# Float32 bits of the float64 weights built in a contiguous tile, mask constants loaded first, and 96-row value loads, in an attention-plus-two-mixtures kernel

## The chip, the cores and the metric

One NeuronCore of a Trainium2 chip runs the whole kernel as one launch. The metric is device time in microseconds (us): the time of one execution, as the median of three runs. The engines are TensorE (PE, matrix products), VectorE (DVE), ScalarE (ACT), GpSimd (POOL) and SyncE (SP, which here only issues DMAs).

## The reference

Three stages follow one another. First sparse attention over 4 batches, 8 heads, 576 positions and head width 64; heads 0 to 3 see a band of 32 positions (local), heads 4 to 7 see every 32nd position (strided). Then a gated two-layer product with float64 weights, and then a mixture of eight experts of which each token uses two. Cut to what matters:

```python
mask_local = (rel >= 0) & (rel < stride)
mask_strided = (rel >= 0) & (pos[None, :] % stride == pos[:, None] % stride)
attn = softmax(np.where(mask, scale * q @ k.T, -1e9))     # per head
x = (attn @ v).transpose(0, 2, 1, 3).reshape(2304, 512)
h = x @ w_in                                   # 512 x 2048, float64
x = (h * (1.0 / (1.0 + np.exp(-1.702 * h)))) @ w_out      # 2048 x 512, float64
# second mixture: 8 experts of 512 x 1024 and 1024 x 512, top 2 of noisy logits per token
out[mask] += top2_w[mask, k, None] * (np.maximum(x[mask] @ w1[e], 0.0) @ w2[e])
```

## The kernel before

The 2304 tokens run in six chunks of 384 (`c`). A prologue loop (lines 698 to 712) computes most of the first batch's attention; then the loop over `(c, fc)` (lines 747 to 797) runs the first mixture with 16 slices of 128 hidden units (`fc`) for each chunk, and works on attention groups of later chunks and on other tasks in between. From line 801 on, the second mixture runs per expert. In the first part the order on PE, ACT, DVE and POOL is the order in which the program writes the instructions (`manual_schedule`, lines 118 and 682); only the order of SP's DMA issues is left to the scheduler.

**The float64 weights.** Each piece of 128x512 float64 weights is loaded as pairs of 32-bit words into `raw` (`w_raw`, called `area` or `raw` in the trace; four such buffers). `w_bits` makes float32 bits of it with three DVE instructions: line 387 shifts and masks the high words into a tile `cv`; line 390 shifts the low words and joins them with `cv`, written back over the low words, that is into every second word of `raw`; line 393 adds sign and exponent bits, again into every second word. Then `w_split` makes two float32r parts: ACT copies the result (line 362, the high part), POOL subtracts (line 363, the low part). The `cv` tile has one buffer and is free after line 390. `raw` is free after line 363. Wide pieces have 512 columns (28 of them); the last two `fc` have eight pieces of 256 columns.

**How the pieces pass.** `w_step` is a generator: each `next(conv)` lets out the next of the three DVE instructions. One `fc` iteration of chunk 0 holds two such steps, the first half (lines 758 to 769) and the second half (lines 770 to 795). Each half ends with `w_split`, which issues the ACT copy and the POOL subtraction of the step before the one just finished (`SPLIT` holds two lists). So the POOL subtraction of step k stands at the end of step k+1, and line 387 of step k+2 is the next DVE instruction of a step after it. In the prologue only every second pass holds a step (`CONVAT`), while every pass calls `w_split`.

**Order on the engines in one iteration of chunk 0.** DVE: line 387 (first half), line 418 (gate product, from PSUM), line 193 (low part of attention values), line 390, line 169 (masked scores, two), line 393; line 387 (second half), line 178, line 390, line 180 (normalisation), line 393. POOL: line 425 (low part of the gate), line 363 of the last second-half step, line 182 (normalised probabilities), line 363 of this iteration's first-half step. ACT: line 416 (tanh), line 190, line 423 (high part of the gate), line 174 (exponents), line 362, line 240 (copy of the transposed probabilities), line 362.

**Loads and constants.** `chained` (line 138) gives DMAs to SP one behind another. The constants `cs` (128x738 float32: identity, local masks, strided mask and others) are one DMA, second in the queue, between the first group's `qk` and its `v`. A local group's `v` is a 128x384 load of which the product reads 96 rows (line 252). A tile `zero` of 128x512, filled by POOL at line 720 ahead of chunk 0, is the source with which `clear` writes zeros to DRAM during chunks 3 and 4.

Of the kernel before, what the change touches and what calls it, by code (L numbers as in the profile page):

```python
# [9 lines left out]
F32 = mybir.dt.float32  # L10
F32R = mybir.dt.float32r
BF16 = mybir.dt.bfloat16
I32 = mybir.dt.int32
# [9 lines left out]
DM = H * D  # L23
# [32 lines left out]
WAIT1 = 15  # L56
R_PP = R_LG + 16 * TPC

C_ID = 0
C_ML = C_ID + 128  # L60
C_MS = C_ML + 2 * KW
C_TRI = C_MS + 128
C_TOK = C_TRI + 128
C_EB = C_TOK + NT
# [33 lines left out]
def tile_kernel(ctx, tc, qkL, qkS, vL, vS, wm1, wm2, wgn, noise, cst, lst0, out):  # L98
# [19 lines left out]
    with ExitStack() as main, tc.manual_schedule(engines={mybir.EngineType.PE}):  # L118
# [13 lines left out]
        def xtile(c):  # L132
            X[c] = xtp.tile([128, 2, 4, CH], F32R, tag="xt", name=f"xt{c}")

        # ---------------- attention
        LASTLD = {}

        def chained(dst, src, late=False):
            prev = LASTLD.get(late) or LASTLD.get(False)
            if prev is None:  # L140
                ins = nc.sync.dma_start(dst, src).ins
            else:
                with tc.issue_after(prev):
                    ins = nc.sync.dma_start(dst, src).ins
            LASTLD[late] = ins

        def attn_load(gr, early):
            b, pr, g = gr
            if early:
                area = wp.tile([128, 2048], F32, tag="w", name="att")  # L150
                qk, v = area[:, :QKL], area[:, QKL:QKL + 384].rearrange("p (t d) -> p t d", d=128)
                p, pt = area[:, 1024:1408], area[:, 1408:1792]
            else:
                qk = ldp.tile([128, QKL], F32, tag="qk", name="qk", bufs=2)
                v = ldp.tile([128, 3, 128], F32, tag="v", name="v", bufs=3)
                p = pt = None
            if pr < 2:
                chained(qk, qkL[b, pr, g], not early)
                if (b, pr, g) == (0, 0, 0):
                    chained(cs, cst)  # L160
                chained(v, vL[b, pr, g].rearrange("p (t d) -> p t d", d=128), not early)
            else:
                chained(qk[:, :QKS], qkS[b, pr - 2, g], not early)
                chained(v[:, 0, :], vS[b, pr - 2, g], not early)
            return qk, v, p, pt
# [108 lines left out]
            put_x(parts, conv)  # L274

        class Attention:
            """Groups in order, each in four stages; a group starts once it lies below `limit`."""

            def __init__(self, gs, early, pooled):
                self.gs, self.early, self.pooled = gs, early, pooled  # L280
# [36 lines left out]
                    g_av(self.gs[i], self.ld[i], self.pt.pop(i), banks[i % len(banks)], conv)  # L317
                    self.done += 1

        # ---------------- float64 weights: bits -> float32 -> two float32r parts  # L320
        W1 = {}

        PIECES, SMALL, held, born, done, slot = [], [], [], [], [], {}
        SPLIT = [[], []]

        def w_raw(fc, s):
            """Load a part of the weights of fc and, with the first, make room for the result."""
            if fc >= NFC:
                return
            wide = fc < NFC - 2  # L330
            if wide:
                if not s:
                    slot[fc] = wslot(f"w1_{fc}")
                w = slot[fc][:, :, 512 * s:512 * s + 512]
            else:
                w = rap.tile([128, 2, 512], F32R, tag="ra", name=f"w1_{fc}_{s}")
            W1[fc, s] = w[:, 0, :], w[:, 1, :]
            if wide:
                raw = rap.tile([128, 512, 2], I32, tag="ra", name="area")
                chained(raw.rearrange("p n t -> p (n t)"), wm1[fc, :, 512 * s:512 * s + 512].bitcast(I32))  # L340
                PIECES.append((fc, s, raw, 0, 512))
            else:
                SMALL.extend((fc, s, o, 256) for o in (0, 256))
# [12 lines left out]
                born.append(len(done))  # L356

        def w_split():
            """float32r parts of what the step before converted"""
            for fc, s, w32, o, n in SPLIT.pop(0):  # L360
                hi, lo = W1[fc, s]
                nc.scalar.copy(hi[:, o:o + n], w32)
                nc.gpsimd.tensor_sub(lo[:, o:o + n], w32, hi[:, o:o + n].bitcast(F32))
                if n < 512:
                    held.pop()
                else:
                    w_raw(fc + 2, s)
            w_small()
            SPLIT.append([])
            done.append(0)  # L370

        def w_step():
            left = 512
            while PIECES and left:
                fc, s, raw, o, n = PIECES[0]
                if n < 512:
                    if len(done) < born[0] + LATE:
                        return
                    born.pop(0)
                PIECES.pop(0)  # L380
                left -= n
                yield from w_bits(fc, s, raw, o, n)

        def w_bits(fc, s, raw, o, n):
            t = tmp.tile([128, n], I32, tag="cv", name="cv", bufs=1)
            low, high = raw[:, :, 0], raw[:, :, 1]
            nc.vector.tensor_scalar(t, high, 3, 0x3FFFFFFF,
                                    op0=OP.logical_shift_left, op1=OP.bitwise_and)
            yield
            nc.vector.scalar_tensor_tensor(low, low, 29, t,  # L390
                                           op0=OP.logical_shift_right, op1=OP.bitwise_or)
            yield
            nc.vector.scalar_tensor_tensor(low, high, -0x40000000, low,
                                           op0=OP.bitwise_and, op1=OP.bitwise_or)
            SPLIT[-1].append((fc, s, low.bitcast(F32), o, n))
            yield

        # ---------------- first mixture: two products with a gated activation
        GT = {}
        LASTMM = [None]  # L400

# [35 lines left out]
                m = nc.tensor.matmul(o, g[:, 1, a], w[0], start=False, stop=(fc == NFC - 1))  # L437
            LASTMM[0] = m.ins

        # ---------------- routing  # L440
        scat = []

        def routing(c, tb, lb, wait=3):
# [72 lines left out]
            nc.tensor.matmul(ps, ones, mc, start=True, stop=False)  # L516
            nc.tensor.matmul(ps[:, :TPC], tri, mb[:, :TPC], start=False, stop=True)
            nc.scalar.copy(pp, ps)
            # weights of the two experts
            pay = one.tile([128, TPC, 2, 2], F32, tag="pay", name="pay", bufs=2)  # L520
            sc = one.tile([128, 8, TPC], F32, tag="sc", name="sc")
            for k in range(2):
# [6 lines left out]
            nc.vector.tensor_scalar(sc[:, 3], sc[:, 2], 1.0, 1e-9, op0=OP.add, op1=OP.add)  # L529
            nc.vector.reciprocal(pay[:, :, 0, 1], sc[:, 3])  # L530
            nc.vector.tensor_mul(pay[:, :, 1, 1], sc[:, 2], pay[:, :, 0, 1])
            # places in the experts' lists
            pos, t1 = sm[:, 10], sm[:, 11]
            nc.vector.tensor_add(pos, pp[:, :TPC], base[:, None, :].to_broadcast([128, TPC, E]))
            nc.vector.tensor_add(base, base, pp[:, TPC])
# [15 lines left out]
                    scat.append(s)  # L551
            yield

        # ---------------- second mixture: per expert
        W2 = {}

        def w2_load(h):
# [112 lines left out]
                    tc.declare_no_dep(s.ins, o.ins, reason="an expert's tokens are distinct")  # L670
                adds[e].append(s)

        # ================= program
        def groups(b, loc):
            return [(b, pr, g) for pr in (0, 1, 2, 3) for g in (loc if pr < 2 else range(NG))]

# [39 lines left out]
        nc.vector.memset(ones, 1.0)  # L716
        nc.vector.tensor_copy(base, cs[:, C_EB:C_EB + E])

        z = one.tile([128, DM], F32, tag="zero", name="zero")
        nc.gpsimd.memset(z, 0.0)  # L720

        def clear(t, r0, n):
            src = bass.AP(tensor=z.tensor, offset=z.offset, ap=[list(z.ap[0]), [0, n], [1, DM]])
            chained(t[r0:r0 + 128 * n, :].rearrange("(b p) d -> p b d", p=128), src, True)

        fill = []

        def step(n=1):
            for _ in range(n):
# [18 lines left out]
        for i, (c, fc) in enumerate(seq):  # L748
            if fc == 0:
                if c:  # L750
                    drain()
                for k in {2: (3, 4), 3: (5,)}.get(c, ()):
                    xtile(k)
                if 0 < c < len(parts):
                    finish(c)
                if c + 1 < len(parts):
                    att.limit = upto[c + 1]
            conv = w_step()
            t, g = m1_l1(c, fc, step, conv)
            att.values([7])  # L760
            att.transposes([6])
            next(conv, None)
            att.scores([5])
            next(conv, None)
            m1_split(c, t, g)
            att.exps()
            for _ in conv:
                pass
            w_split()
            conv = w_step()  # L770
            att.norms(conv)
            if c == 3 and fc in (4, 6, 8, 10, 12):
                clear(x2d, 64 * fc - 256, 1)
            if c == 0 and fc == 12:
                chained(lst.rearrange("(p n) t -> p (n t)", p=128),
                        lst0.rearrange("(p n) t -> p (n t)", p=128), True)
            if c == 4 and fc % 2:
                clear(out, CH * (fc // 2), min(TPC, NT + NBLK - TPC * (fc // 2)))
            if c == NCHUNK - 1 and fc == 6:
                drain()  # L780
                e_list(0, 0, NA // 128)
                fill.append(e_part(0, 0, N + DUMP - CH, wait=WAIT0))
            if c == NCHUNK - 1 and fc >= 8:
                w2_load(fc - 8)
            if i:
                m1_l2(*seq[i - 1], step)
                if fc == 0:
                    fill.insert(0, routing(c - 1, [6], 7))
            att.values([7], conv)
            next(conv, None)  # L790
            att.transposes([6])
            att.load()
            for _ in conv:
                pass
            w_split()
            if (c, fc) == (NCHUNK - 2, NFC - 1):
                fine.close()
# [49 lines left out]
                m2_l2(h, (t,))  # L847
            e_out(E - 1, (t,))

        # ---------------- blocks beyond the fixed capacity  # L850
        ov = one.tile([1, 6, E], F32, tag="ov", name="ov")
        oi = one.tile([1, E], I32, tag="oi", name="oi")
        nc.vector.tensor_sub(ov[:, 0], base[0:1], cs[0:1, C_EB:C_EB + E])
# [119 lines left out]
```

## Time and profile before

| | us |
|---|---|
| median of three runs | 1048.15 |
| lowest and highest of three | 1048.09, 1048.95 |
| span of the profiled execution | 1046.7 |
| PE busy | 999.4 (95%) |
| DVE busy | 498.7 (48%) |
| ACT busy | 394.7 (38%) |
| POOL busy | 233.0 (22%) |

The profile is of one execution; its span, from the first to the last instruction, lies 1.45 us under the median. Busy times are totals over stages with different limits, so they are read stage by stage: by windows of time, by the order of instructions in one loop iteration, and by what each engine waited for. A busy instruction on DVE or POOL can be one that has started and stands still; its duration against the shortest of its kind shows that.

### The profile page before, as it was taken

To read this page: it belongs to the slowest core of one execution; us is meant where nothing else is said; L and a number is where in the kernel's file an instruction comes from. 1 tells how busy PE (TensorE), PEld (TensorE's weight loads), DVE (VectorE), ACT (ScalarE), POOL (GpSimd) and SP (SyncE) were. 2 spreads that over 40 slices of the span, in tenths; PEclk is the share of its full clock that TensorE was granted. 3 is DMA by queue.
4 is the path that set the end of the run, shared out by engine and by line. 5 is a ranking of instruction groups with operands and counts; after the bars stand their busy time and mean duration, and the time that the engine had idled before them with its cause. 6 is when DMAs were issued, how large, how long until landed. Compare 5 with 4: busy or idle time off the path is not lost. (4 is left out here: it accounts for less than half of the span.)

```text
span 1046.7 us, 16112 instructions
## 1 busy us (share of the span) xinstructions
PE 999.4 (95%) x5804; PEld 884.2 (84%) x5804; DVE 498.7 (48%) x1509; ACT 394.7 (38%) x1075; POOL 233.0 (22%) x210
## 2 busy tenths in 40 slices
PE   6898799999999999999989999999999999999996
PEld 5776688998888888889978779998999998999995
DVE  5999955236544744522553454343434334343311
ACT  5754444234435444322343153242423323233311
POOL 2577630200200200110210333032220405031302
PEclk9699999999999999999989999999999999999998
DMA  8656521011212223400050065253452726253403
GB/s 278 217 179 191 188 73 48 1 62 46 51 53 87 78 88 129 180 1 31 31 188 34 19 183 153 81 118 124 88 155 81 164 78 145 97 132 111 93 9 51
DMA packets 64352, 107.69 MB, mean 103 GB/s; under 512 B 13056, under 2 KB 26496, under 8 KB 64256
## 3 DMA queue, kind: packets, MB, share of 16 engines
q1 hardware_dynamic: 54160, 85.64, 25.4%
q0 software_dynamic: 10112, 21.02, 10.1%
q8 instruction: 46, 0.75, 0.3%
q14 instruction: 34, 0.28, 0.1%
HBM read 84.04 MB, written 22.73 MB: 102 GB/s over the span
## 5 line engine op out<-in xcount | busy, mean ns | idle before, releaser
L638 DVE SCALAR_TENSOR_TENSOR ht<-pb,ht 128x384 fp32r<-128x384 f32 (+1 forms) x128 | 62.5, 488 | 254.9 <-ACT ht L637 254.9
L637 ACT ACTIVATE ht<-pb 128x384 fp32r<-128x384 f32 (+1 forms) x128 | 56.0, 438 | 264.7 <-PE pb L636 264.6
L411 PE MATMUL pb<-xt,w 128*128 128x384 f32 x384 | 135.8, 354 | 0.0
L666 POOL DMA_INDIRECT out<-y,ix x40 | 65.3, 1633 | 290.4 <-ACT y L665 260.9
L412 PE MATMUL pb<-xt,w 128*128 128x384 f32 x384 | 129.5, 337 | 0.1
L413 PE MATMUL pb<-xt,w 128*128 128x384 f32 x384 | 129.6, 337 | 0.0
L435 PE MATMUL pb<-w,g 128*128 128x512 f32 x288 | 121.1, 420 | 7.5 <-ACT g L423 7.5
L650 PE MATMUL pb<-w,ht 128*128 128x512 f32 x320 | 127.8, 399 | 0.0
L651 PE MATMUL pb<-w,ht 128*128 128x512 f32 x320 | 125.3, 392 | 0.0
L652 PE MATMUL pb<-w,ht 128*128 128x512 f32 x320 | 125.1, 391 | 0.0
L546 POOL DMA_INDIRECT lst<-pay,si x36 | 36.2, 1004 | 399.1 <-DVE si L543 338.6
L418 DVE SCALAR_TENSOR_TENSOR th<-th,pb 128x384 f32<-128x384 f32 x96 | 52.9, 551 | 148.9 <-ACT th L416 148.8
L437 PE MATMUL pb<-w,g 128*128 128x512 f32 x288 | 115.8, 402 | 0.6 <-POOL g L425 0.6
L436 PE MATMUL pb<-w,g 128*128 128x512 f32 x288 | 114.8, 399 | 0.0
L416 ACT ACTIVATE th<-pb 128x384 f32<-128x384 f32 x96 | 47.0, 490 | 140.7 <-PE pb L413 138.6
L564 DVE TENSOR_TENSOR w<-raw,w 128x512 fp32r<-128x512 f32 x128 | 83.9, 688 | 15.7 <-ACT w L563 15.3
L634 PE MATMUL pb<-xa,w 128*128 128x384 f32 x256 | 87.2, 340 | 0.0
L636 PE MATMUL pb<-xa,w 128*128 128x384 f32 x256 | 86.3, 337 | 0.0
L635 PE MATMUL pb<-xa,w 128*128 128x384 f32 x256 | 86.0, 336 | 0.0
L423 ACT CAST g<-th 128x384 fp32r<-128x384 f32 x96 | 49.3, 513 | 87.7 <-DVE th L418 87.5
L563 ACT CAST w<-raw 128x512 fp32r<-128x512 f32 x128 | 73.9, 617 | 16.3 <-DMA raw<-wm 16.2
L412 PEld LDWEIGHTS pb<-xt,w 128*128 128x128 f32 x384 | 72.9, 190 | 2.5 <-DVE st L178 0.4
(167 smaller groups left out, 1999.0 us busy)
## 6 DMA issues: line engine op xcount, KB each, us to landing
raw<-wm SPq DMA_DIRECT2D x136, 256.0 KB, 3.0
area<-wm SPq DMA_DIRECT2D x28, 512.0 KB, 4.0
out<-zero SPq DMA_DIRECT2D x7, 768.0 KB, 6.9
qk<-qkS SPq DMA_DIRECT2D x28, 189.0 KB, 2.8
qk<-qkL SPq DMA_DIRECT2D x16, 304.0 KB, 2.9
x2d<-row SPq DMA_DIRECT2D x15, 256.0 KB, 2.2
v<-vL SPq DMA_DIRECT2D x16, 192.0 KB, 2.4
att<-qkL SPq DMA_DIRECT2D x8, 304.0 KB, 6.2
```

The costliest lines, as they stand in the source:

```text
L411: nc.tensor.matmul(ps, w[0][:, a], X[c][:, 0, kc, :], start=(kc == 0), stop=False)
L412: nc.tensor.matmul(ps, w[0][:, a], X[c][:, 1, kc, :], start=False, stop=False)
L413: nc.tensor.matmul(ps, w[1][:, a], X[c][:, 0, kc, :], start=False, stop=(kc == 3))
L435: nc.tensor.matmul(o, g[:, 0, a], w[0], start=(fc == 0), stop=False)
L436: nc.tensor.matmul(o, g[:, 0, a], w[1], start=False, stop=False)
L437: m = nc.tensor.matmul(o, g[:, 1, a], w[0], start=False, stop=(fc == NFC - 1))
L634: nc.tensor.matmul(ps, w[:, 0, a], x[:, 0, kc, :], start=(kc == 0), stop=False)
L635: nc.tensor.matmul(ps, w[:, 0, a], x[:, 1, kc, :], start=False, stop=False)
L636: nc.tensor.matmul(ps, w[:, 1, a], x[:, 0, kc, :], start=False, stop=(kc == 3))
L650: nc.tensor.matmul(o, g[:, 0, a], w[:, 0, 512:], start=(fc == 0), stop=False)
L651: nc.tensor.matmul(o, g[:, 0, a], w[:, 1, 512:], start=False, stop=False)
L652: m = nc.tensor.matmul(o, g[:, 1, a], w[:, 0, 512:], start=False, stop=(fc == NF2 - 1))
```

## The change

- `w_step` takes one `cv` tile of 128x512 for a step, from two buffers that take turns (the pool's default) where there was one. `w_bits` writes all three results into a contiguous slice of that tile. `raw` is only read, by DVE. The ACT copy and the POOL subtraction read the `cv` tile, so it is in use until line 363's subtraction is done, and `raw` until the third DVE instruction.
- The local masks stand first in `cs`; their columns load ahead of the first `v`, the other columns behind it, in a DMA of their own.
- A local group's `v` loads 96 rows.
- The `zero` tile becomes a `cv` tile, filled at the start of chunk 3.
- Comments and blank lines go.

```diff
-C_ID = 0
-C_ML = C_ID + 128
-C_MS = C_ML + 2 * KW
+C_ML = 0
+C_ID = C_ML + 2 * KW
+C_MS = C_ID + 128
...
                 if (b, pr, g) == (0, 0, 0):
-                    chained(cs, cst)
-                chained(v, vL[b, pr, g].rearrange("p (t d) -> p t d", d=128), not early)
+                    chained(cs[:, :C_ID], cst[:, :C_ID])
+                chained(v[:KW], vL[b, pr, g, :KW].rearrange("p (t d) -> p t d", d=128), not early)
+                if (b, pr, g) == (0, 0, 0):
+                    chained(cs[:, C_ID:], cst[:, C_ID:])
...
             for fc, s, w32, o, n in SPLIT.pop(0):
-                hi, lo = W1[fc, s]
-                nc.scalar.copy(hi[:, o:o + n], w32)
-                nc.gpsimd.tensor_sub(lo[:, o:o + n], w32, hi[:, o:o + n].bitcast(F32))
+                hi, lo = (w[:, o:o + n] for w in W1[fc, s])
+                nc.scalar.copy(hi, w32)
+                nc.gpsimd.tensor_sub(lo, w32, hi.bitcast(F32))
...
-            left = 512
+            left, t = 512, None
...
+                if t is None:
+                    t = tmp.tile([128, 512], I32, tag="cv", name="cv")
+                yield from w_bits(fc, s, raw, o, n, t[:, 512 - left:512 - left + n])
                 left -= n
-                yield from w_bits(fc, s, raw, o, n)
-
-        def w_bits(fc, s, raw, o, n):
-            t = tmp.tile([128, n], I32, tag="cv", name="cv", bufs=1)
+
+        def w_bits(fc, s, raw, o, n, w32):
             low, high = raw[:, :, 0], raw[:, :, 1]
-            nc.vector.tensor_scalar(t, high, 3, 0x3FFFFFFF,
+            nc.vector.tensor_scalar(w32, high, 3, 0x3FFFFFFF,
                                     op0=OP.logical_shift_left, op1=OP.bitwise_and)
             yield
-            nc.vector.scalar_tensor_tensor(low, low, 29, t,
+            nc.vector.scalar_tensor_tensor(w32, low, 29, w32,
                                            op0=OP.logical_shift_right, op1=OP.bitwise_or)
             yield
-            nc.vector.scalar_tensor_tensor(low, high, -0x40000000, low,
+            nc.vector.scalar_tensor_tensor(w32, high, -0x40000000, w32,
                                            op0=OP.bitwise_and, op1=OP.bitwise_or)
-            SPLIT[-1].append((fc, s, low.bitcast(F32), o, n))
+            SPLIT[-1].append((fc, s, w32.bitcast(F32), o, n))
...
-        z = one.tile([128, DM], F32, tag="zero", name="zero")
-        nc.gpsimd.memset(z, 0.0)
...
+                if c == 3:
+                    ZERO.append(tmp.tile([128, DM], F32, tag="cv", name="zero"))
+                    nc.gpsimd.memset(ZERO[0], 0.0)
```

## Rows read from the trace of the kernel before

**Rows 1.** The page: the span, and DVE's busy tenths in 40 slices of the span (26 us each).

```profile
span 1046.7 us, 16112 instructions
...
DVE  5999955236544744522553454343434334343311
```

**Rows 2.** Busy time of each engine in two stretches: most of chunk 0, and from the end of chunk 0 to the end of the span. Columns: stretch, its length, busy us (instructions) of PE, PE's weight loads, DVE, ACT, POOL, granted clock, DMA share, GB/s.

```profile
46.00:126.00 80.00, 68.41 (x417) 56.60 (x416) 79.03 (x173) 40.92 (x128) 57.79 (x47) 0.98 0.56 182
...
142.00:1046.00 904.00, 883.66 (x5118) 789.15 (x5116) 372.66 (x1151) 318.40 (x804) 148.04 (x126) 0.99 0.32 88
```

**Rows 3.** The timeline of DVE and POOL in one iteration of chunk 0. Columns: start us, duration us, engine, line, operation, tiles, shapes, count, and in brackets the idle time before it with what ended it.

```profile
69.04 0.42 DVE L387 TENSOR_SCALAR cv<-area 128x512 int32<-128x512 int32 x1
...
69.38 0.15 DVE L178 TENSOR_SCALAR st<-st 126x2 f32<-126x2 f32 x1
69.45 1.30 POOL L363 TENSOR_TENSOR w<-area,w 128x512 fp32r<-128x512 f32 x1 [0.88 <-ACT w L362]
...
69.56 1.73 DVE L390 SCALAR_TENSOR_TENSOR area<-area,cv 128x512 int32<-128x512 int32 x1
...
71.22 0.15 DVE L180 RECIPROCAL st<-st 126x2 f32<-126x2 f32 x1
...
71.33 0.69 DVE L393 SCALAR_TENSOR_TENSOR area<-area 128x512 int32<-128x512 int32 x1
71.45 1.04 POOL L182 TENSOR_TENSOR psd<-psd,st 126x252 f32<-126x252 f32 x1 [0.70 <-DVE st L180]
...
71.94 0.83 DVE L387 TENSOR_SCALAR cv<-area 128x512 int32<-128x512 int32 x1
...
72.45 1.50 POOL L363 TENSOR_TENSOR w<-area,w 128x512 fp32r<-128x512 f32 x1
...
72.69 0.54 DVE L418 SCALAR_TENSOR_TENSOR th<-th,pb 128x384 f32<-128x384 f32 x1
...
73.16 0.45 DVE L193 TENSOR_TENSOR xt<-pb,xt 128x42 fp32r<-128x42 f32 x2
...
73.50 0.99 DVE L390 SCALAR_TENSOR_TENSOR area<-area,cv 128x512 int32<-128x512 int32 x1
...
73.90 1.47 POOL L425 TENSOR_TENSOR g<-th,g 128x384 fp32r<-128x384 f32 x1
...
74.42 0.28 DVE L169 CUSTOM_DVE_ANT_0 psd<-pb,cs 126x126 f32<-126x126 f32 x1
```

**Rows 4.** The same iteration's end: DVE's timeline, and the POOL subtraction that closes it.

```profile
74.84 1.08 DVE L393 SCALAR_TENSOR_TENSOR area<-area 128x512 int32<-128x512 int32 x1
75.84 0.41 DVE L387 TENSOR_SCALAR cv<-area 128x512 int32<-128x512 int32 x1
...
76.25 1.30 POOL L363 TENSOR_TENSOR w<-area,w 128x512 fp32r<-128x512 f32 x1 [0.88 <-ACT w L362]
```

**Rows 5.** Timelines of DVE and POOL: the first and the last line 387 of chunk 0's steps whose counterpart two steps back is still running on POOL, and that counterpart, line 363.

```profile
51.73 0.62 DVE L387 TENSOR_SCALAR cv<-area 128x512 int32<-128x512 int32 x1
...
120.20 1.78 DVE L387 TENSOR_SCALAR cv<-raw 128x256 int32<-128x256 int32 x1
...
52.03 1.48 POOL L363 TENSOR_TENSOR w<-area,w 128x512 fp32r<-128x512 f32 x1
...
120.53 1.30 POOL L363 TENSOR_TENSOR w<-area,w 128x512 fp32r<-128x512 f32 x1
```

**Rows 6.** All instructions of one line over the whole span. Columns: engine, operation, tiles, count, shortest, median and longest ns, first and last start, shapes. Lines 390, 393 and 363 work on every second word of `raw`; lines 425 and 564 on contiguous tiles.

```profile
L390 DVE SCALAR_TENSOR_TENSOR area<-area,cv x28: 675/1082/1831, 14.5 to 118.9; 128x512 int32<-128x512 int32 x28
...
L393 DVE SCALAR_TENSOR_TENSOR area<-area x28: 692/694/1194, 15.2 to 119.6; 128x512 int32<-128x512 int32 x28
...
L564 DVE TENSOR_TENSOR w<-raw,w x128: 679/691/694, 518.9 to 989.1; 128x512 fp32r<-128x512 f32 x128
...
L363 POOL TENSOR_TENSOR w<-area,w x28: 1291/1306/1504, 18.2 to 124.0; 128x512 fp32r<-128x512 f32 x28
...
L363 POOL TENSOR_TENSOR w<-raw,w x8: 742/773/919, 125.5 to 141.0; 128x256 fp32r<-128x256 f32 x8
...
L425 POOL TENSOR_TENSOR g<-th,g x16: 998/1458/1472, 48.2 to 143.8; 128x384 fp32r<-128x384 f32 x16
```

**Rows 7.** Who waited for whom, 0 to 160 us, on SP (us in total, times, longest); and the timeline row of the first conversion, with the one wait of line 387 for its data.

```profile
SPq L144 <- POOL w L363: 70.2, 23, 7.7
...
13.70 0.43 DVE L387 TENSOR_SCALAR cv<-area 128x512 int32<-128x512 int32 x1 [0.81 <-DMA area<-wm]
```

**Rows 8.** The start: PE's wait for the second group's `qk` in the timeline, the size of a local group's `v` load in the list of DMA issues (KB each, median us from issue to landing), and the DMA rate between 6 and 8 us (columns as in rows 2).

```profile
7.59 4.35 PE L206 MATMUL pb<-att 128*128 128x96 f32 x18 [2.49 <-DMA att<-qkL]
...
att<-vL SPq DMA_DIRECT2D x8, 192.0 KB, 6.1
...
6.00:8.00 2.00, 0.41 (x2) 0.41 (x3) 0.00 (x0) 0.77 (x5) 0.00 (x0) 1.00 1.03 371
```

**Rows 9.** The end of chunk 0's conversions: a line 387 on DVE, and on POOL the three merged subtractions of which the second is its counterpart two steps back.

```profile
131.34 1.10 DVE L387 TENSOR_SCALAR cv<-raw 128x256 int32<-128x256 int32 x1
...
132.25 2.37 POOL L363 TENSOR_TENSOR w<-raw,w 128x256 fp32r<-128x256 f32 x3
```

**Rows 10.** PE's longest idle time inside chunk 0's strided groups, and the granted clock just after it (columns as in rows 2).

```profile
90.71 0.35 PE L262 MATMUL pb<-pt,v 72*64 72x72 f32 x4 [2.14 <-ACT pt L240]
...
92.00:94.00 2.00, 2.00 (x6) 1.56 (x6) 2.00 (x5) 0.00 (x0) 1.35 (x2) 0.50 0.49 152
```

More of the change, by code (lines that the diff above doesn't have):

```diff
@@ L717, in tile_kernel @@
         nc.vector.tensor_copy(base, cs[:, C_EB:C_EB + E])
-        z = one.tile([128, DM], F32, tag="zero", name="zero")
-        nc.gpsimd.memset(z, 0.0)
         def clear(t, r0, n):
+            z = ZERO[0]
             src = bass.AP(tensor=z.tensor, offset=z.offset, ap=[list(z.ap[0]), [0, n], [1, DM]])
             chained(t[r0:r0 + 128 * n, :].rearrange("(b p) d -> p b d", p=128), src, True)
-        fill = []
+        fill, ZERO = [], []
         def step(n=1):
```

## The prediction

> **What bounds the kernel now.** I read the share of busy time by stretches first, then the order of instructions in one loop iteration, then the shortest and median durations of single lines, and last the waits. The share alone says "PE, 95%"; the slices say more: DVE is at nine tenths or above from slice 2 to slice 5, roughly 26 to 130 us, and at half after that [rows 1]. In 46 to 126 us DVE is busy 79.03 of 80 us, while PE, whose busy time includes overlapping matmuls, has 68.41; from 142 us on PE is busy 884 of 904 us [rows 2]. So the kernel has a first part whose pace DVE sets and a second whose pace PE sets. A delay in the first part starts the second later, and nothing there can take it back.
>
> What the reader is to see in one iteration of the first part [rows 3, 4]: its period is 76.25 - 69.45 = 6.80 us, and DVE has no gap, but several of its instructions stand still. Line 390 takes 1.73 us at 69.56 though its shortest run is 0.68 [rows 6]: POOL's line 363 runs to 70.75, and line 390 ends 0.54 later. Line 387 at 71.94 ends 0.28 after POOL's line 182; the next line 390 (0.99) ends 0.54 after POOL's line 363. The other way round, line 182 at 71.45 ends 0.47 after DVE's line 393. Such DVE and POOL instructions take turns. While POOL subtracts, DVE goes on only with what needs no turn: lines 418 and 193 run through POOL's 72.45 to 73.95.
>
> **Part 1, the contiguous tile: what it removes.** Strided operands seem to cost DVE nothing: line 393 on every second word has a median of 694 ns, line 564 on contiguous tiles 691, both 128x512 [rows 6]. On POOL the line through 742 ns (256 columns) and 1291 (512) gives 1017 at 384; the contiguous line 425 has 998 at its shortest [rows 6]. The gain is 0.02 us a subtraction, and I put it at nothing. `raw` comes free after DVE's third instruction instead of POOL's subtraction, so SP issues weight loads earlier; SP waited 70.2 us on line 363 for that, but the converting line 387 waited for data just once, 0.81 us at 13.70, before any buffer is used again [rows 7]. Nothing.
>
> **What it adds.** The result stays in the `cv` tile until POOL has subtracted, and there are two such tiles. So line 387 of step k+2 must wait for line 363 of step k. In program order that subtraction is issued only at the end of step k+1, and line 387 of step k+2 is DVE's next conversion. In the rows, line 387 at 69.04 starts 1.71 us before its counterpart ends (69.45 + 1.30), the one at 71.94 starts 2.01 before the other ends (72.45 + 1.50) [rows 3]. The first such pair is 51.73 against 52.03 + 1.48, the last 120.20 against 120.53 + 1.30 [rows 5]: two waits an iteration, ten iterations. In the prologue a pass without conversion lies between, in which POOL subtracts, so I count none. Queued behind the waiting line 387 on DVE are the normalisation (lines 178, 180), which POOL's line 182 waits for, and line 418, which ACT's line 423 and then POOL's line 425 wait for.
>
> **The new period, step by step**, from T, the end of the second-half step's counterpart on POOL (70.75 in the rows); hand-over 0.08 (line 180 ends 71.37, line 182 starts 71.45), all from [rows 3, 4] and unblocked lengths from [rows 6]:
> - line 387 at T+0.08; line 390 0.52 after it begins (69.04 to 69.56), 0.69 long, ends T+1.29 (now T+0.54, since line 387 had run under the subtraction);
> - line 393 0.04 later, 0.69 long: T+2.02; line 182, blocked by it, 0.47 more: T+2.49;
> - line 363 of the first half starts 0.04 before that and takes 1.30 with no DVE in its way: T+3.75;
> - only now the next line 387, T+3.83, 0.42 long; line 418 starts 0.08 before it ends: T+4.17; line 390 starts 0.81 after line 418: T+4.98; ends T+5.67 (now T+3.74);
> - from there to the next line 363 as now, 76.25 - 74.49 = 1.76 (masks, exponents, ACT's copy): T+7.43; its 1.30: T+8.73.
>
> 8.73 instead of 6.80 is 1.93 us an iteration: the work that ran under POOL's subtractions, lines 387, 418 and 193, now follows them. Bounds: 1.4, if line 182 gets its turn before line 393 (saves about 0.45) and the hand-over is shorter; 2.4, if line 393 of the first half, which ends about 0.3 ahead of line 363 in this count, slips in front of it. I take 1.93, which follows the program order.
>
> Sum over the stage: the first waiting line 387 ends at 52.03 + 1.30 + 0.08 + 0.42 = 53.83 (now 52.35). Ten periods later it is 141.1; less 0.8, an estimate, for two iterations whose group has 72 rows instead of 126 [rows 10]: 140.3. Now that instruction ends at 120.20 + 1.78 = 121.98 [rows 5]. So +18.3 us. In the tail, line 387 at 131.34 would wait for the second of three subtractions that start at 132.25, till about 133.8 [rows 9]: 0 to 1.4 us; I take 0.3, nearer to nothing, since the last slices' products come later.
>
> **Part 2, masks first.** The first group's masks come earlier, but PE waits for the second group's `qk` until 7.59, which stands behind the same constants [rows 8]. Nothing; bounds 0 to 0.5 us of gain, and up to 0.5 of loss by one more issue on SP, hidden as long as the DMA rate is the limit (share 1.03 [rows 8]).
>
> **Part 3, 96 rows.** A local `v` is 192 KB and becomes 144. Four such loads stand ahead of the first weights: 4 x 48 KB at 371 GB/s [rows 8] is 0.5 us, which shortens the 0.81 us that line 387 waited at 13.70 [rows 7]. I take -0.5, bounds 0 and -0.8. Later `v` loads are waited for by nobody. [...] No trace so far shows a 96-row load.
>
> **Part 4, the zero tile.** POOL's fill moves to chunk 3, into a tile that conversions left long before; POOL is busy 148 of the last 904 us [rows 2], which hides it. Without that cover it would cost what it takes, about half a us.
>
> **Sum.** 1046.7 + 18.3 + 0.3 - 0.5 = 1064.8 us of span [rows 1]; the median lies 1.45 above the span of the profiled run: 1066.2.
>
> **The rivals.**
> [...]
> - *No wait binds*: the tile gets more room than I read, or the wait lands elsewhere. Then only part 3 remains: 1047.6. Against it: the pool's default is two buffers.
> - *Faster:* contiguous operands speed POOL's subtraction up. Place: the two line 363 of an iteration. It decides from the point at which they save 1.93 us, 0.97 each, that is at 0.33 us instead of 1.30; at 0.2 us it would gain 0.27 ten times, less 0.5: 1045. Against it: 0.02 in [rows 6].
>
> **How the numbers follow.** Forecast 0.72 (1060 to 1072 from the bounds 1.4 and 2.4 and the tail), clock 0.16, no wait 0.09, faster 0.03. About 0.2%, 2 us, is what a measurement of this kernel can tell from no change. Slower is 0.72 + 0.16 = 0.88; the no-wait case is two thirds within it, so same 0.06, faster 0.06. The range 1058 to 1079 leaves out the last two cases and reaches to the clock's price.
>
> **What would show it.** Right: DVE idle at line 387 with POOL's line 363 as releaser, about twenty times, some 1.8 us each; the period near 8.7; line 390's median near 0.7 instead of 1.08; chunk 0 ending some 18 us later, and the rest as long as now. Wrong: no such idle time; subtractions far under 1.29 us; or a lower granted clock with PE as releaser, which would be the rival.

## The result

| | before | after |
|---|---|---|
| median, us (4 runs each) | 1048.16 | 1062.97 |
| lowest and highest, us | 1048.09, 1048.95 | 1061.81, 1064.15 |
| span of the profiled execution, us | 1046.7 | 1062.0 |
| DVE busy, us | 498.7 | 478.9 |

The change makes the kernel slower: the ratio is 1.0137, 95% interval 1.0125 to 1.0149, or 14.8 us. The forecast was 1066.2 within 1058 to 1079, slower. One run of e2 below took 1951.75 us and is left out of e2's median, which is of the three others. Lines have moved: 387, 390, 393 (the three conversions) are 390, 393, 396 after; the ACT copy is 364, the subtraction 365; the normalisation's lines are 180, 182, 184; the gate product on DVE is 421.

The page of the kernel after, span and DVE's tenths; the counterpart is [rows 1]:

```profile
span 1062.0 us, 16117 instructions
...
DVE  5956664524744654532444545343333334343311
```

The four nines of slices 2 to 5 are gone, and the kernel is slower. A DVE that is "less busy" here is one that waits on a semaphore where it stood still inside an instruction or worked before. The list of waits for 0 to 170 us (us in total, times, longest) has the new row that the prediction asked for:

```profile
DVE cv L390 <- POOL w L365: 36.6, 22, 2.3
```

22 waits of 1.66 us on average (forecast: about twenty of some 1.8). The timeline of DVE and POOL in one iteration of chunk 0 (start, duration, engine, line, in brackets the idle time before it and what ended it), to be laid beside [rows 3, 4]:

```profile
66.31 1.27 POOL L365 TENSOR_TENSOR w<-cv,w 128x512 fp32r<-128x512 f32 x1 [0.85 <-ACT w L364]
67.62 0.43 DVE L390 TENSOR_SCALAR cv<-area 128x512 int32<-128x512 int32 x1 [1.60 <-POOL w L365]
...
68.08 0.69 DVE L393 SCALAR_TENSOR_TENSOR cv<-area,cv 128x512 int32<-128x512 int32 x1
...
68.81 0.69 DVE L396 SCALAR_TENSOR_TENSOR cv<-area,cv 128x512 int32<-128x512 int32 x1
68.93 1.04 POOL L184 TENSOR_TENSOR att<-att,st 126x252 f32<-126x252 f32 x1 [1.34 <-DVE st L182]
69.92 1.28 POOL L365 TENSOR_TENSOR w<-cv,w 128x512 fp32r<-128x512 f32 x1
71.23 0.43 DVE L390 TENSOR_SCALAR cv<-area 128x512 int32<-128x512 int32 x1 [1.74 <-POOL w L365]
71.58 0.55 DVE L421 SCALAR_TENSOR_TENSOR th<-th,pb 128x384 f32<-128x384 f32 x1
...
72.39 0.69 DVE L393 SCALAR_TENSOR_TENSOR cv<-area,cv 128x512 int32<-128x512 int32 x1
...
73.41 1.07 DVE L396 SCALAR_TENSOR_TENSOR cv<-area,cv 128x512 int32<-128x512 int32 x1
74.78 1.27 POOL L365 TENSOR_TENSOR w<-cv,w 128x512 fp32r<-128x512 f32 x1 [0.85 <-ACT w L364]
76.09 0.43 DVE L390 TENSOR_SCALAR cv<-area 128x512 int32<-128x512 int32 x1 [1.61 <-POOL w L365]
```

Each line 390 starts 0.03 to 0.04 us after a subtraction ends, where line 387 had started 1.7 to 2.0 us before the end of its counterpart [rows 3]. DVE stands idle through both subtractions, and lines 421 and 195, which had run under one, follow it. The period is 76.09 - 67.62 = 8.47 us (before 6.80).

All instructions of one line over the whole span (shortest, median, longest ns), to be laid beside [rows 6]:

```profile
L393 DVE SCALAR_TENSOR_TENSOR cv<-area,cv x28: 680/693/1753, 15.0 to 135.3; 128x512 int32<-128x512 int32 x28
...
L365 POOL TENSOR_TENSOR w<-cv,w x36: 722/1272/1623, 20.3 to 158.4; 128x512 fp32r<-128x512 f32 x28, 128x256 fp32r<-128x256 f32 x8
```

The middle conversion's median fell from 1082 to 693 ns: it no longer stands still behind a subtraction, since it can't start before one is over. The subtraction on contiguous words lost some 0.03 us: 1.27 to 1.28 in the iteration above, 1.30 where nothing stood in its way before [rows 3, 4].

Busy time by stretches, columns as in [rows 2]:

```profile
46.00:126.00 80.00, 61.36 (x359) 49.58 (x358) 50.00 (x149) 35.19 (x114) 42.66 (x38) 0.94 0.48 157
...
80.00:90.00 10.00, 7.54 (x43) 5.99 (x41) 6.65 (x21) 3.88 (x12) 4.95 (x5) 1.00 0.46 160
90.00:100.00 10.00, 6.98 (x31) 5.51 (x31) 6.58 (x21) 4.85 (x18) 5.44 (x6) 0.83 0.40 132
...
158.00:1061.00 903.00, 882.00 (x5119) 786.80 (x5117) 372.75 (x1151) 319.11 (x804) 149.56 (x129) 1.00 0.32 88
```

In 46 to 126 us all engines do less: PE 61.36 us of work instead of 68.41, DVE 50.00 busy instead of 79.03. After chunk 0 nothing has changed (PE 882 of 903 us, before 884 of 904).

Where the time came from is read on the gate product (line 421), the first, sixteenth and seventeenth of the kernel after:

```profile
47.92 0.56 DVE L421 SCALAR_TENSOR_TENSOR th<-th,pb 128x384 f32<-128x384 f32 x1 [0.52 <-ACT th L419]
...
159.00 0.56 DVE L421 SCALAR_TENSOR_TENSOR th<-th,pb 128x384 f32<-128x384 f32 x1 [2.24 <-ACT th L419]
...
163.07 0.56 DVE L421 SCALAR_TENSOR_TENSOR th<-th,pb 128x384 f32<-128x384 f32 x1 [3.51 <-ACT th L419]
```

Before, they start at 46.79, 142.58 and 146.76. So 1.1 us of the difference lies ahead of chunk 0, and chunk 0 (first to seventeenth) takes 115.15 us instead of 99.97: 15.2 of the 15.3 us by which the spans differ. From there to the end it is 898.9 us after and 899.9 before.

### The profile page after: what moved, and what is told of

The parts are those of the page before. It is cut to its first block, busy times and chain, and to the rows that moved or that the text cites. A ratio compares the mean times of both kernels' runs of the same rounds, so it can differ in the third digit from the quotient of the medians.

```text
span 1062.0 us, 16117 instructions
## 1 busy us (share of the span) xinstructions
PE 1003.6 (95%) x5804; PEld 885.5 (83%) x5804; DVE 478.9 (45%) x1509; ACT 393.8 (37%) x1075; POOL 227.5 (21%) x210
## 5 line engine op out<-in xcount | busy, mean ns | idle before, releaser
L438 PE MATMUL pb<-w,g 128*128 128x512 f32 x288 | 122.4, 425 | 8.8 <-ACT g L426 8.8
L440 PE MATMUL pb<-w,g 128*128 128x512 f32 x288 | 116.9, 406 | 0.2 <-POOL g L428 0.2
L439 PE MATMUL pb<-w,g 128*128 128x512 f32 x288 | 116.0, 403 | 0.0
```

Of the source, the lines that this page charges most:

```text
L438: nc.tensor.matmul(o, g[:, 0, a], w[0], start=(fc == 0), stop=False)
L439: nc.tensor.matmul(o, g[:, 0, a], w[1], start=False, stop=False)
```

## The experiments

The theory: the `cv` tiles bind (two tiles, each in use until POOL has subtracted), through the wait of line 390. The rivals: another part of the change, or the wait is only a sign and DVE and POOL lose the time to each other anyway. All ratios are to the kernel before on the same chip, with 95% intervals. "Chunk 0" is the time from the first to the seventeenth gate product.

**e1: more tiles.** The kernel after, but the converted words of most pieces get tiles of other pools, so that no line 390 waits for a subtraction.

```diff
-                    t = tmp.tile([128, 512], I32, tag="cv", name="cv")
+                    pool, tag = (stp, "raw") if fc < 12 else (tmp, "row") if fc == 12 else (tmp, "cv")
+                    t = pool.tile([128, 512], I32, tag=tag, name="cv")
```

> The changed kernel with more room for the contiguous bits: steps of the first twelve weight slices take their tile from three buffers that small pieces use later, the thirteenth from two others, so that no tile is used again until three steps later; nothing else differs. If the added time is the wait of VectorE for GpSimd's subtraction, that wait (36.6 us in 22 waits) falls to a few us and the time to 1047 to 1051 us. If the contiguous tile itself costs (its writes, its reads, the earlier loads), the time stays above 1058 us though the waits are gone.

Measured: 1048.67 us, ratio 0.9994 [0.998, 1.0008]; chunk 0 100.48 us. Its waits of DVE, 0 to 170 us (line 391 is the first conversion here):

```profile
DVE cv L391 <- POOL w L365: 3.8, 2, 2.3
```

Two waits are left of 22. With the rest of the change in place, the whole loss is gone. In its timeline the first conversion again starts before POOL's subtraction for the step two back is over (here 0.5 us before it begins), and the middle one stands still behind that subtraction as before (it ends 0.54 us later):

```profile
66.14 0.83 DVE L391 TENSOR_SCALAR cv<-area 128x512 int32<-128x512 int32 x1
66.65 1.47 POOL L365 TENSOR_TENSOR w<-cv,w 128x512 fp32r<-128x512 f32 x1
...
67.70 0.96 DVE L394 SCALAR_TENSOR_TENSOR cv<-area,cv 128x512 int32<-128x512 int32 x1
```

**e2, e3, e4: one part each.** e2 is the kernel after with masks and `v` as before; e3 is the kernel before with the masks first; e4 is the kernel before with 96 rows of `v`. The edits are the lines of the diff above.

> The kernel before with the contiguous two-buffer tile and the moved zero tile alone; masks and 128-row value loads as before. Theory of the wait: chunk 0 takes the same 15 us longer, and the start loses nothing: 1060.5 to 1063 us. If the masks or the 96 rows share in the loss beyond the start, it is below 1059 us.

> The kernel before with the local masks first and the constants in two DMAs, nothing else. If this edit makes the first 20 us 1.1 us longer, the time is 1049 to 1049.7 us and PE's second group starts near 8.0 us instead of 7.59; if it is the 96-row loads, 1048.2 us and 7.6 us.

> The kernel before with 96-row value loads of local groups, nothing else. By bytes (four loads of 48 KB less ahead of the first weights) 1047.7 us, with the first converting instruction 0.5 us earlier. If 96 rows fill no faster than 128, 1048.2 us. If the loss at the start is theirs, 1049 to 1049.7 us.

Measured: e2 1064.07 us, 1.0154 [1.0129, 1.0179], chunk 0 115.24 with the same 22 waits of 36.6 us in all. That is 1 us above the range expected, and far from the rival's, below 1059. e3 1049.41, 1.0004 [0.9993, 1.0015], with PE's second group at 7.45 us. e4 1048.62, 0.9999 [0.9989, 1.0009], with that group at 7.75. The tile alone is the whole loss; the other two parts are nothing that can be measured. Whether they share in the 1.1 us at the start can't be told (first gate product at 47.45 us in e3, 47.14 in e4, 46.79 before).

What e4 shows of the load, first the rate between 6 and 8 us, then the local `v` in its list of DMA issues (KB, us from issue to landing); the counterparts are in [rows 8].

```profile
6.00:8.00 2.00, 0.25 (x1) 0.25 (x2) 0.00 (x0) 0.83 (x6) 0.00 (x0) 1.00 1.05 297
```

```profile
att<-vL SPq DMA_DIRECT2D x8, 144.0 KB, 6.8
```

In the kernels that load 96 rows the rate in this window is lower: 297 GB/s at a share of 1.05 in e4, 293 at 0.98 in the kernel after and 310 at 1.00 in e1, where it was 371 at 1.03 before and 379 in e2 and e3. Loads of 128 rows are in the queue in the same window (in the kernel after, SP issues a `qk` at 4.47 and one at 5.80 us, and a local `v` at 5.02 between them), and the time from issue to landing is longer there than later: the 144 KB landed after 6.8 us in e4 and after 6.1 in the kernel after, the 192 KB after 6.1 in the kernel before, while the 16 later loads of a local `v` landed after 2.2 us in e4 and in the kernel after, and 2.4 in the kernel before. So the bytes of a local `v` fell by a quarter, and the rate in this window by a fifth in e4. Whether the smaller load saves anything stays open: the interval of e4 reaches 1 us to either side, and its first conversion, at 13.14 us without a wait for data, lies among those of kernels with 128 rows (13.04 in e2, 13.70 before). No run here has a window of 96-row loads alone.

**e5: the wait one instruction later.** The kernel after, but the first conversion writes a tile of its own (`tw`) and only the second one writes `cv`. So DVE waits one conversion later, where the kernel before stood still too.

```diff
-            nc.vector.tensor_scalar(w32, high, 3, 0x3FFFFFFF,
+            t = w32
+            if fc < 13:
+                pool, tag = (stp, "raw") if fc < 12 else (tmp, "row")
+                t = pool.tile([128, 512], I32, tag=tag, name="tw")
+            nc.vector.tensor_scalar(t, high, 3, 0x3FFFFFFF,
...
-            nc.vector.scalar_tensor_tensor(w32, low, 29, w32,
+            nc.vector.scalar_tensor_tensor(w32, low, 29, t,
```

> The changed kernel, but the first of the three converting instructions writes into a tile of its own that is free after the second, as in the kernel before; only the second and third write the contiguous two-buffer tile. The wait for GpSimd's subtraction so moves by one instruction, from the first to the second, for the pieces of the first thirteen weight slices. My theory says that what costs is not the wait as such but the work that used to run under the subtraction (the first instruction, the normalisation, the gate product): the second instruction stood still until that same subtraction's end before, too. Then 1047 to 1051 us, with waits of VectorE for GpSimd still in the trace, at the second instruction. If any wait on the tile costs what it lasts, 1056 us or more.

Measured: 1058.84 us, 1.0084 [1.0064, 1.0105]; chunk 0 110.81, period 7.87. A miss: by my theory the second conversion had to stand behind the subtraction anyway, so that a wait there would cost next to nothing. Only some 6 of the 15 us came back. The timeline of e5 (lines 394, 397, 400 are the conversions, 425 and 432 the gate product and its low part) shows why:

```profile
81.34 1.28 POOL L365 TENSOR_TENSOR w<-cv,w 128x512 fp32r<-128x512 f32 x1 [2.25 <-ACT w L364]
82.65 0.69 DVE L397 SCALAR_TENSOR_TENSOR cv<-area,tw 128x512 int32<-128x512 int32 x1 [1.58 <-POOL w L365]
...
84.49 1.47 POOL L365 TENSOR_TENSOR w<-cv,w 128x512 fp32r<-128x512 f32 x1
...
85.95 1.01 POOL L432 TENSOR_TENSOR g<-th,g 128x384 fp32r<-128x384 f32 x1
86.00 1.52 DVE L397 SCALAR_TENSOR_TENSOR cv<-area,tw 128x512 int32<-128x512 int32 x1 [0.35 <-POOL w L365]
```

An instruction that had begun and stood still ended 0.54 us after POOL [rows 3]. Released by the semaphore, it starts 0.03 after POOL's end and needs its full 0.69: 0.18 more. The second one loses far more: POOL's next instruction, line 432, begins 0.05 us earlier and goes first, and line 397 takes 1.52. It ends at 87.52, 1.56 after the subtraction (85.96): 1.0 us more than one that had stood in line. Together with the first half this is 1.2 us, about the 7.87 - 6.80 = 1.07 by which the period is longer.

**e6: the subtraction one step earlier.** The kernel after, but `w_split` issues copy and subtraction of a step at the end of the same step.

```diff
-        SPLIT = [[], []]
+        SPLIT = [[]]
```

> The changed kernel with the ACT copy and the GpSimd subtraction of a step issued at the end of that step and not of the next. The subtraction of step k is then over long before the first instruction of step k+2. Theory of the wait: VectorE's waits for GpSimd go; the price is that ACT stands at its copy until VectorE's third instruction is done, behind it the copy of the transposed probabilities that PE waits for: 1048 to 1056 us. If the wait of VectorE were not the cause, above 1060 us.

Measured: 1046.44 us, 0.9968 [0.9954, 0.9982]: faster than both kernels. Chunk 0 takes 100.12, its period is 6.75, and no wait of DVE for POOL is left. With the two tiles kept and only the place of the copy and the subtraction in the order moved (and of the load that is issued with them), the loss is gone, so it was not contiguity, nor the number of instructions. The time also lies below the 1048 to 1056 us expected: ACT does stand before its copy (1.86 us before the one at 70.93), but chunk 0 does not get longer by that (100.48 in e1).

**e7: what the turns cost in the kernel before.** The kernel before with a second ACT copy in place of the subtraction, so that it leaves out the true low part.

```diff
-                nc.gpsimd.tensor_sub(lo[:, o:o + n], w32, hi[:, o:o + n].bitcast(F32))
+                nc.scalar.copy(lo[:, o:o + n], w32)
```

> The kernel before, but the low part of each weight piece is a second ACT copy instead of GpSimd's subtraction, so the low part holds another value than the reference needs. Its time shows what taking turns with GpSimd costs VectorE in chunk 0. By the rows of before VectorE stands still 2.14 of 6.80 us in an iteration (1.04 + 0.41 + 0.30 + 0.39); without the subtractions only GpSimd's two other instructions are left. If taking turns sets the pace: the second converting instruction falls to 0.69 us, the period to about 5.4 us, where PE's products begin to bound, and the time to 1032 to 1038 us. If the strided operand made it slow: 1048 us and still 1.08 us at the median.

Measured: 1027.12 us, 0.9779 [0.9758, 0.9799]; chunk 0 83.19, period some 5.5. Its window of 46 to 126 us:

```profile
46.00:126.00 80.00, 78.02 (x454) 66.32 (x453) 69.02 (x188) 59.86 (x168) 27.25 (x26) 1.00 0.59 186
```

PE is now busy 78.02 of 80 us: with the subtractions away from POOL, the bound passes from DVE to PE. The gain, 23 us by the medians, is larger than I had expected. The turns that DVE takes with POOL's subtractions are what sets chunk 0's pace in the kernel before.

**e8: the subtraction on DVE.** The same line on `nc.vector`.

> The kernel before with the subtraction of the weights' low part on VectorE instead of GpSimd; it computes the same. If taking turns sets the pace, VectorE's 4.66 us of own work in an iteration grow by two times 0.69 to 6.0, plus up to 0.7 for the two GpSimd instructions left: 6.0 to 6.7 us instead of 6.80, so 1040 to 1047 us, faster than both kernels. If VectorE's work alone is the bound and the standing still hides nothing, 8.2 us and 1062 us.

Measured: 1047.61 us, 0.9974 [0.9961, 0.9987]; chunk 0 97.29. Its period is 6.95 us and not 6.0 to 6.7, and the time is 0.6 us above the range expected. In each iteration DVE waits some 0.28 us for ACT's copy, which I had not counted, and twice an instruction takes 0.4 us more than its shortest (line 363 here, and line 393 with 1.08 at 75.65, against 0.69), which I put down to the two instructions that POOL has left:

```profile
70.06 0.69 DVE L363 TENSOR_TENSOR w<-area,w 128x512 fp32r<-128x512 f32 x1 [0.28 <-ACT w L362]
...
72.46 1.10 DVE L363 TENSOR_TENSOR w<-area,w 128x512 fp32r<-128x512 f32 x1
```

So in these iterations a subtraction on DVE itself costs about what standing still behind POOL's costs. What chunk 0 won lies outside them; the two iterations whose group has 72 rows, for one, last 6.66 and 6.50 us instead of 7.82 and 7.69.

**e9: the early split without the tile.** The edit of e6 on the kernel before.

> The kernel before with one edit: the split of a step is issued at the end of that same step instead of at the end of the next (the list holds one entry at the start instead of two). Theory A, the early split alone is what made e6 faster than the kernel before: ratio 0.995 to 0.998, 1045 to 1048 us. Theory B, the contiguous tile is needed for that gain (raw free earlier, nothing in place): 1.000, 1049 to 1050. By both, DVE still has no idle time at line 387 with POOL as releaser.

Measured: 1047.29 us, 0.9978 [0.9965, 0.9991]. So the early split alone is faster than the kernel before too; the interval overlaps that of e6, and whether the tile adds anything stays open. What the profiles show of the gain lies in the prologue. There the subtraction runs in the pass that holds a conversion in the kernel before; in e9 it starts in the other one and reaches only into the next first conversion. The subtraction and the middle conversion of a pass in the kernel before, then the subtraction, the first and the middle conversion in e9 (timelines of DVE and POOL):

```profile
28.11 1.29 POOL L363 TENSOR_TENSOR w<-area,w 128x512 fp32r<-128x512 f32 x1 [0.60 <-ACT w L362]
...
28.13 1.82 DVE L390 SCALAR_TENSOR_TENSOR area<-area,cv 128x512 int32<-128x512 int32 x1
```

```profile
25.21 1.30 POOL L363 TENSOR_TENSOR w<-area,w 128x512 fp32r<-128x512 f32 x1
...
25.82 0.98 DVE L387 TENSOR_SCALAR cv<-area 128x512 int32<-128x512 int32 x1
...
27.14 0.68 DVE L390 SCALAR_TENSOR_TENSOR area<-area,cv 128x512 int32<-128x512 int32 x1
```

The middle conversion takes 1.82 against 0.68 us, the first one 0.59 (at 27.20) against 0.98. From the second to the sixth first conversion it is 37.06 - 17.37 = 19.69 us in the kernel before, 34.37 - 17.04 = 17.33 in e9, 35.79 - 18.56 = 17.23 in e6 and 37.88 - 18.41 = 19.47 in the kernel after. In e9's profile chunk 0 itself is longer (102.77), and what follows it shorter (897.9) than before (899.9), so the profile bears out the prologue's 2.4 us but not the sum.

**e10: the normalisation on ACT.** The kernel of e6, but ACT normalises the probabilities from the second batch on, instead of POOL.

```diff
+            if pool == 2:
+                for t in range(nt):
+                    nc.scalar.mul(p[:q, t, :w], p[:q, t, :w], st[:q, 2, t:t + 1])
+                return
...
-                    normalize(*self.sm[self.nb], self.nb < self.pooled, conv)
+                    normalize(*self.sm[self.nb], 0 if self.nb >= self.pooled else 2 if self.nb >= upto[0] else 1, conv)
```

> The kernel of e6 with one edit: in chunk 0, from the second batch on, ACT normalises the probabilities (one multiplication by a per-row scale for each tile) instead of POOL, so that POOL has one instruction less per iteration for which it takes turns with DVE. Theory A, taking turns with POOL sets the pace of chunk 0 once no wait binds: 0.4 to 0.6 us an iteration, 1041 to 1045 us. Rival: ACT's instructions come in order, so its two multiplications delay exponents and weight copies behind them and eat the gain: 1046 or more.

Measured: 1050.83 us, 1.0006 [0.9994, 1.0017]. No gain, and some 4 us behind e6 (medians of two chips). Its period is 6.74 (e6 6.75) and its chunk 0 99.90 (100.12): the pace hasn't moved, though POOL is busy 43.38 of 80 us in 46 to 126, where it was 56.66. The chain is elsewhere. In the timeline of e10 (368 copy, 369 subtraction, 400 third conversion):

```profile
73.80 1.46 POOL L369 TENSOR_TENSOR w<-cv,w 128x512 fp32r<-128x512 f32 x1 [1.28 <-ACT w L368]
...
74.17 1.64 DVE L400 SCALAR_TENSOR_TENSOR cv<-area,cv 128x512 int32<-128x512 int32 x1
...
75.84 0.62 ACT L368 CAST w<-cv 128x512 fp32r<-128x512 f32 x1 [0.59 <-DVE cv L400]
...
76.54 1.30 POOL L369 TENSOR_TENSOR w<-cv,w 128x512 fp32r<-128x512 f32 x1 [1.28 <-ACT w L368]
76.88 0.56 DVE L425 SCALAR_TENSOR_TENSOR th<-th,pb 128x384 f32<-128x384 f32 x1 [0.74 <-ACT th L423]
...
78.12 1.14 POOL L432 TENSOR_TENSOR g<-th,g 128x384 fp32r<-128x384 f32 x1 [0.29 <-POOL w L369]
...
78.73 1.08 DVE L400 SCALAR_TENSOR_TENSOR cv<-area,cv 128x512 int32<-128x512 int32 x1
...
80.55 1.45 POOL L369 TENSOR_TENSOR w<-cv,w 128x512 fp32r<-128x512 f32 x1 [1.28 <-ACT w L368]
```

In the first half the third conversion stands behind the subtraction (it ends 0.55 us later), then comes ACT's copy of it. In the second half tanh (line 423) follows that copy on ACT, then the gate product (425), its high part on ACT (77.47 to 77.99), its low part on POOL (432), a third conversion that stands behind it (it ends 0.55 us later), ACT's copy and the next subtraction: 80.55 - 73.80 = 6.75 us, the whole period, and the normalisation has no part in it. My reason for the gain was wrong, and the rival's reason is not shown either: the loss lies ahead of chunk 0, whose first gate product starts at 49.63 us (e6 44.57). ACT's three normalisations of the last prologue passes stand there (0.90 to 0.91 us each, at 40.93, 43.89 and 47.95), but that they cost it was only argued; the cause stays open.

## Why the prediction was right, and by how much it was off

**Mechanism.** Right at each step: line 387 (now 390) waits for line 363 (365) of the step before the last; 22 waits; all of the time in chunk 0; e1 (tiles) and e6 (order) each remove wait and loss by different edits, and e2, the tile alone, has both. In the prologue no wait was counted and none came, but not for the reason given. The subtraction does not run in the pass without a conversion: in the kernel before, the one at 28.11 runs beside a middle conversion (under e9). No wait comes because the first conversion two steps on starts only at 32.24 us, 2.84 after that subtraction's end.

**The sum.** 18.3 us was forecast for the stage. Counted as there, the last waiting first conversion ends at 138.29 + 0.29 = 138.58, 16.6 us later than the 121.98 of before, and 1.1 of that is the later start of this execution. The step that was mis-sized is the new period: 8.73 forecast, 8.47 measured. Laid beside the prediction's list, from T = 66.31 + 1.27 = 67.58:

| from T, us | forecast | measured |
|---|---|---|
| line 393 (was 390) ends | 1.29 | 1.19 |
| line 396 (was 393) ends | 2.02 | 1.92 |
| line 184 ends | 2.49 | 2.39 |
| first subtraction ends | 3.75 | 3.62 |
| next line 390 starts | 3.83 | 3.65 |
| line 421 starts | 4.17 | 4.00 |
| second line 393 ends | 5.67 | 5.50 |
| next subtraction ends | 8.73 | 8.47 |

No step is out of order; a few small terms are. The hand-over from POOL to DVE is 0.03 to 0.04 us and not the 0.08 that I had taken from the other direction (DVE to POOL); the gap from the first conversion to the second is shorter by 0.06; the subtraction is 1.27 to 1.28 and not 1.30, twice; and the way from the second conversion to the next subtraction has 0.06 less, as ACT's copy took 0.60 to 0.62 instead of 0.65. 0.26 us ten times is 2.6 of the 3.2 us by which the median was off. That the rest comes so close is luck: the start came 1.1 us later than before and the time behind chunk 0 was 1.0 shorter, neither of which was forecast.

**The other terms.** The tail (+0.3): the wait was there (2.27 us before 150.30), but the sixteenth gate product came 16.4 us later than before, no more than the conversion ahead of the tail (16.6): nothing. The 96 rows (-0.5): e4 shows no gain that can be told from nothing, and its rate was lower than the 371 GB/s that the term was worked out with. Masks and zero tile (0): e3 and e2 agree. In the kernel after, the second group's `qk` came at 8.04 us instead of 7.59, so nothing was won there.

**The rivals.** PE's clock, to which the forecast gave 0.16, did fall: 0.94 on average in 46 to 126 us (0.98 before), with 0.83 in some stretches of ten us and 1.00 in others; in 94 to 96 us it is 0.50. But the iterations at either are alike. Counted from gate product to gate product, those that start at 71.58, 80.04 and 96.67 us take 8.46, 8.50 and 8.48, with mean clocks of 0.80, 1.00 and 1.00; the one at 88.54, of 72 rows, takes 8.13 at 0.79. So it cost nothing that the wait hadn't taken already. The upper end of the range, 1079, counts with a low clock that makes PE set the period; no run shows that price, and these four periods stand at 8.13 to 8.50 at either clock. No wait binding and a faster subtraction were wrong: 22 waits, 0.03 us.

## What to carry to other kernels

Count a buffer's life to its last reader. When a result moves from a tile that another wait already covered into one of a small rotation, the rotation must cover the distance to that reader in program order: here a third tile's worth of room, or the reader one step earlier, was worth all 15 us. Then ask which work had run under the reader; that, and not the wait's length, is the loss (here 36.6 us of waits cost 15 us). And where two engines take turns, ask whether an instruction has been issued and stands in line or still waits for a semaphore: here line 390 of the kernel before, which stood in line, ended 0.54 us after POOL's subtraction, and line 397 of e5, which waited, 1.56 us after it.

## What the runs showed that I had not expected

- A semaphore wait at the very place where DVE stood still anyway is not free: e5 lost its turn to POOL's next instruction, 1.56 us after the subtraction's end against 0.54.
- With loads of 96 of 128 rows in the queue, the rate in 6 to 8 us was 293 to 310 GB/s (the kernel after, e4, e1) instead of 371 to 379.
- The first matmuls are slow for a time that differs from one execution to the next, while the granted clock reads 1.00 (14 to 16 us in the kernel before and in the kernel after). In the kernel after, PE's 4 matmuls of line 223 take 1.05 us at 15.84; in e6, 0.60 at 15.93. In e2, whose loads are those of the kernel before, the first gate product starts at 45.50 us, in the kernel before at 46.79. So the 1.1 us at the start of the kernel after is within what such starts differ by; its cause stays open.
